# Attention and max-out FFN on one core: key tile 2 of batch 0 in one score group, whole value products, and batch 2's loads one pair later

## The chip, the cores and the metric

One core of a Trainium2 chip runs the whole program. The metric is the device time of one execution in microseconds (us). Engines are named as in the profile: PE multiplies matrices, ACT applies functions, DVE and POOL do elementwise work, SP issues transfers; POOL and ACT can issue transfers too.

## What is computed

Attention with 16 extra "beacon" keys and values in front, then a feed-forward network (FFN) whose hidden layer is the maximum of three products. B, H, S, Nb, D are 8, 8, 576, 16, 64; the FFN is 512 to 768 to 512 over 4608 tokens.

```python
k_all = concatenate([beacon_k, k], axis=2)       # 592 keys
v_all = concatenate([beacon_v, v], axis=2)
scores = matmul(q, k_all.T) / sqrt(D)            # causal over the 576, beacons always seen
a = exp(scores - scores.max(-1)); a /= a.sum(-1) + 1e-9
x = matmul(a, v_all)                             # heads side by side: (4608, 512)
h = maximum(maximum(x @ w1, x @ w2), x @ w3)
out = h @ w_out
```

## The kernel before, in words

**Tiling.** Two heads make a pair; there are four pairs per batch and 32 in all, and two pairs make a quad, whose four heads fill the 128 output partitions 32 by 32. The 592 keys are five tiles of 128 (the last has 80). Scores are kept transposed, keys on partitions, queries on columns; key tile t meets only queries from `q_min[t]` on (0, 112, 240, 368, 496). `exp` is taken without subtracting the maximum, the triangle of a tile is masked to zero, and a value product gives, for each quad, three "parts": part 0 multiplies by ones and gives the sums, parts 1 and 2 are the even and odd value columns. A part's columns from HEAD (64) to 576 fill one bank of 512 columns of the accumulator memory; its first 64 columns go to a shared fourth bank (`pv_heads`).

**Order of work.** The order is written out by hand; every engine runs its own instructions in that order. `first_batch` interleaves, for batch 0, the turning of queries and keys (`T`, L424), scores and their exps (`S_`, L506 and L515), masks (`M`, L563 on DVE), value products (`P`, i.e. `pv_rest`, L592) and the normalization: sums are inverted on ACT as Ln and Exp (`invert_rest`, L633, L634), for the first 64 columns on DVE (L628), and DVE multiplies (L639, L648) into `xT`, the FFN's input. Then the FFN's first units follow (`F_in`, L763). Batch 0's columns are worked on in halves of 288 (HALF), since its queries and keys are loaded in halves.

In batch 0 each pair has four score groups, a group being what one exp takes (`groups_0`, L70): group 0 holds tiles 2, 1 and 0 of the first half of the queries, groups 1 to 3 the rest. Tile 2 is therefore in two groups: 48 columns in group 0, 288 in group 3. Scores of group 0 run while half of the keys is absent, so those columns of the key tile are set to zero (L196). `EARLY` and `LATE` (L607) are the pieces of a part that `pv_rest` multiplies: tiles 0, 1, 2 for the first half, tiles 0 to 4 for the second.

`second_batch` handles pairs 4 to 7 (batch 1): `emit_burst` computes all four groups of a pair (L521) into pairs of banks chosen by `next_pairs`, exps are L541, masks L565 on POOL. Between them stand FFN units (L733, L750) and the turning of the next pair (L405). At its end `emit_pv_whole` multiplies quad 2 (L684) and ACT copies or inverts its banks (L694, L695, L700, L701); then the list of free banks is reordered: the banks of the sums and of the heads (`late_banks`) go to its end. The loop in `emit_all` then takes pairs 8 to 31 in the same way, with a `plan` of what is cast, stored and loaded at which pair.

**Loads.** Batch 0 and the pairs up to 9 are loaded and cast by POOL's queue (`load_cast`) or by SP into halves; from pair 10 on, and for all values, SP loads into seven staging buffers (`load_pair` L226, `load_v` L300 and L305) and POOL casts (L276, L321). `loads` is a list sorted by the step at which a load is cast. At pair 6, after its masks, `second_batch` takes five entries: the first waits for a small memset on POOL (L224), and the order is pair 10, pair 11, values of batch 2 in two pieces, pair 12. After that each cast releases the next load. Pair 10 is cast at pair 8, pair 11 and the first values at pair 9 (pair 11 first), the second values behind them.

## Time and profile before

| | us |
|---|---|
| three timed runs | 283.8, 285.6, 287.52 (median 285.6) |
| the profiled execution, its own time | 284.03 |
| its span from first to last instruction | 282.2 |
| PE busy in the span | 271.6 |
| ACT busy | 162.8 |
| first FFN matmul of batch 0 (L763) starts | 23.76 |
| last PE work ends | 278.6 |

The granted clock of PE is 0.999. The span is read from the left: up to about 24 us the core fetches its first inputs and works batch 0 with little to overlap; from there PE has FFN units to fill every gap until 278.6 us, and the last output is stored behind it. Times in the timeline are from the span's start.

### The profile page before, as it was taken

Reading aid. Unit: us, or ns where it says so; the run is one execution under the profiler, and the core shown is the slowest. Engines: PE = TensorE matmul, PEld = TensorE weight load, DVE = VectorE, ACT = ScalarE, POOL = GpSimd, SP = SyncE. Lnnn points to the kernel's source line nnn. Section 1 sums busy time; section 2 is a strip of 40 time slices with the busy share of each in tenths; the row PEclk is TensorE's granted clock in tenths of the full one; section 3 lists DMA queues with packets and bytes.
Section 4 is the critical chain, followed back from the end, with each engine's and each line's share of the span. In section 5 each row is a group of like instructions: output and inputs, shape, how many; then the busy total and the mean of one; then the engine's idle time right before and its main releaser. Section 6 shows DMA issues by size and latency. Waiting matters only on the chain.

```text
span 282.2 us, 7689 instructions
## 1 busy us (share of the span) xinstructions
PE 271.6 (96%) x3020; PEld 156.4 (55%) x3050; DVE 171.1 (61%) x307; ACT 162.8 (58%) x307; POOL 133.0 (47%) x273
## 2 busy tenths in 40 slices
PE   7788999999999999999999999999999999999994
PEld 3557765556555555555556886555555554444442
DVE  4885655574837566464737382638363847876872
ACT  4995797978668566756675758585857540000000
POOL 7194378557286946475557655683245300000000
PEclk9999999999999999999999999999999999999999
DMA  8999989989997999999999999979745003003004
GB/s 145 214 180 204 219 159 159 241 200 293 275 205 229 199 241 245 186 249 207 250 194 189 252 243 242 187 161 236 184 105 172 0 2 149 2 1 149 0 0 149
DMA packets 85315, 48.82 MB, mean 173 GB/s; under 512 B 64416, under 2 KB 80032, under 8 KB 85280
## 3 DMA queue, kind: packets, MB, share of 16 engines
q1 hardware_dynamic: 78320, 42.25, 66.7%
q0 software_dynamic: 6544, 5.80, 13.5%
q8 instruction: 23, 0.38, 0.6%
q10 hardware_dynamic: 416, 0.30, 0.4%
q14 instruction: 12, 0.10, 0.1%
HBM read 35.13 MB, written 14.22 MB: 175 GB/s over the span
## 4 chain that ended last, share of the span: by engine, by line
PE 92%; ACT 4%; DVE 2%; issue 1%; DVEq 0%
PE acc L733 46%; PE acc L786 16%; PE acc L684 11%; PE acc L521 8%; PE acc L763 4%; ACT at_sb L515 4%; PE acc L405 2%; PE acc L465 1%; PE acc L592 1%; PE acc L804 0%; PE acc L506 0%; PE acc L424 0%; DVE kT L432 0%; DVE hT L750 0%; DVE busy L184 0%
## 5 line engine op out<-in xcount | busy, mean ns | idle before, releaser
L733 PE MATMUL acc<-xT,w_sb 128*128 128x512 bf16 (+4 forms) x728 | 134.2, 335 | 1.5 <-issue 0.2
L750 DVE TENSOR_TENSOR hT<-hT,acc 128x512 bf16<-128x512 bf16 (+1 forms) x104 | 70.2, 677 | 62.5 <-PE acc L733 55.2
L733 PEld LDWEIGHTS <-w_sb 128*128 128x128 bf16 x752 | 69.8, 98 | 59.5
L565 POOL TENSOR_SCALAR_AFFINE_SELECT at_sb<-at_sb 128x256 bf16<-128x256 bf16 x168 | 61.1, 385 | 81.5 <-ACT at_sb L541 80.8
L541 ACT ACTIVATE at_sb<-acc 128x208 bf16<-128x208 f32 (+3 forms) x140 | 89.6, 735 | 5.2 <-PE acc L521 3.3
L786 PE MATMUL acc<-w_out_sb,hT 128*128 128x512 bf16 (+2 forms) x241 | 48.3, 348 | 0.3
L752 ACT CAST hT<-acc 128x352 bf16<-128x352 f32 x18 | 8.1, 452 | 46.9 <-PE acc L733 46.9
L276 POOL CAST p<-st 96x768 bf16<-96x768 f32 x44 | 35.0, 824 | 0.0
L786 PEld LDWEIGHTS <-hT 128*128 128x128 bf16 x246 | 22.6, 98 | 22.0 <-DVE hT L750 1.9
L793 DVE COPY y<-acc 128x512 f32<-128x512 f32 (+1 forms) x35 | 22.0, 629 | 20.8 <-PE acc L786 15.2
L752 DVE CAST hT<-acc 128x512 bf16<-128x512 f32 (+1 forms) x48 | 26.6, 554 | 9.6 <-PE acc L733 9.1
L811 ACT COPY y<-acc 128x320 f32<-128x320 f32 x1 | 0.4, 426 | 46.0 <-PE acc L804 46.0
L521 PE MATMUL acc<-qT,kT 64*128 64x208 bf16 (+1 forms) x336 | 26.3, 279 | 0.2 <-DVE hT L750 0.2
L684 PE MATMUL acc<-at_sb,v_sb 128*32 128x336 bf16 (+5 forms) x672 | 22.8, 281 | 0.0
L521 PEld LDWEIGHTS <-kT 64*128 64x128 bf16 x336 | 15.4, 94 | 11.5 <-issue 1.1
L711 DVE TENSOR_TENSOR xT<-raw,recip 128x576 bf16<-128x576 f32 x28 | 20.7, 781 | 0.9 <-ACT recip L548 0.9
L321 POOL CAST v_sb<-st 128x1536 bf16<-128x1536 f32 (+2 forms) x21 | 18.3, 897 | 0.0
L684 PEld LDWEIGHTS <-v_sb 128*32 128x32 bf16 (+1 forms) x672 | 14.4, 97 | 6.6
L694 ACT COPY raw<-acc 128x512 f32<-128x512 f32 x28 | 15.7, 633 | 2.8 <-PE acc L684 2.8
L684 PE MATMUL acc<-at_sb,ones 128*32 128x512 bf16 (+3 forms) x336 | 14.9, 284 | 0.0
L515 ACT ACTIVATE at_sb<-acc 128x1024 bf16<-128x1024 f32 (+3 forms) x16 | 12.6, 864 | 0.8 <-PE acc L506 0.8
L763 PE MATMUL acc<-xT,w_sb 128*128 128x256 bf16 x96 | 11.7, 273 | 0.0
(76 smaller groups left out, 174.5 us busy)
## 6 DMA issues: line engine op xcount, KB each, us to landing
out_dram<-y SPq DMA_DIRECT2D x35, 256.0 KB, 3.4
st<-in_q_dram SPq DMA_DIRECT2D x22, 288.0 KB, 4.6
st<-in_k_dram SPq DMA_DIRECT2D x22, 288.0 KB, 5.1
st<-in_v_dram SPq DMA_DIRECT2D x24, 256.0 KB, 5.8
w_sb<-in_moe_w_dram POOLq DMA_DIRECT2D x6, 384.0 KB, 8.6
q_dram<-p SPq DMA_DIRECT2D x16, 144.0 KB, 2.5
k_dram<-p SPq DMA_DIRECT2D x16, 144.0 KB, 2.4
st<-in_v_dram SPq DMA_DIRECT2D x8, 224.0 KB, 6.1
```

The source lines that it names most:

```text
L276: cast(t16.rearrange("p r h d -> p h r d"), st[0:QP, i * NQ2 : (i + 1) * NQ2].rearrange("p (h r d) -> p h r d", h=2, r=QR),)
L515: nc.scalar.activation(out=both_heads(p, gi), in_=ps[:, :, 0 : g_width(p, gi)], func=AF.Exp, scale=scale)
L521: nc.tensor.matmul(ps, kTs[p % NT][hs, 128 * t : 128 * t + 128], qTs[p % NT][hs, q0:q1], start=True, stop=True, tile_position=(64 * e, 0),)
L541: nc.scalar.activation(out=both_heads(p, gi)[:, e0:e1], in_=acc[:, first + e0 : first + e1, 0 : g_width(p, gi)], func=AF.Exp, scale=scale,)
L565: nc.gpsimd.affine_select(out=view, in_=view, compare_op=ALU.is_ge, fill=0.0, base=x0, pattern=[[0, 2], [1, hi - lo]], channel_multiplier=-1,)
L684: nc.tensor.matmul(acc[32 * j : 32 * j + 32, bank, lo + q0 - qa : lo + qb - qa], lhsT, at_view(PPQ * quad + j // 2, t, j % 2, q0, qb), sta ...
L733: nc.tensor.matmul(ps[:, a:b], w_in[i][:, ct, 128 * ft : 128 * (ft + 1)], xT[:, ct, x0 : x0 + b - a], start=(ct == 0), stop=(ct == n_ct - 1),)
L750: nc.vector.tensor_max(h[:, lo:hi], h[:, lo:hi], ps[:, lo:hi])
L752: (by_act if hi < TOKB else by_dve)(h[:, lo:hi], ps[:, lo:hi])
L763: nc.tensor.matmul(ps, w_in[i][:, ct, 128 * (ft + f) : 128 * (ft + f + 1)], xT[:, ct, tb * TOKB + lo : tb * TOKB + hi], start=(ct == 0), s ...
L786: nc.tensor.matmul(ps[:, lo:hi], hT[:, ft, 128 * tt : 128 * (tt + 1)], w_out_sb[:, ft, lo:hi], start=(ft == 0), stop=(ft == n_ft - 1),)
L793: (by_act if hi < d_model else by_dve)(y[:, lo:hi], ps[:, lo:hi])
```

## The change

In batch 0, group 0 keeps tiles 1 and 0 (464 columns a head instead of 512) and group 3 takes tile 2 whole (416 instead of 368); the zeroing of the key columns is gone. `EARLY` and `LATE` are cut anew: tile 0 is one piece of 512 columns, tile 1 two pieces, tiles 2 to 4 one each. In `first_batch` the products follow that: quad 1's parts 1 and 2 are each multiplied whole, with the multiply of that part's early columns behind it, and quad 0's late products of tile 3 and 4 move ahead of quad 1's.

Batch 2's loads are taken at pair 7, after its masks, and no longer at pair 6, and the second cast of batch 1's values goes ahead of them. Their order becomes pair 10, values, pair 11, pair 12, and pair 11 is cast behind both value pieces. The reordering of the banks at the end of `second_batch` is dropped.

```diff
     groups_0 = [
-        [(2, q_min[2], HALF), (1, q_min[1], HALF), (0, 0, HALF)],
+        [(1, q_min[1], HALF), (0, 0, HALF)],
         [(0, HALF, S)],
         [(1, HALF, S), (3, q_min[3], S)],
-        [(2, HALF, S), (4, q_min[4], S)],
+        [(2, q_min[2], S), (4, q_min[4], S)],
     ]
...
-        nc.vector.memset(z[:, Nb + HALF : 384], 0.0)
...
-    EARLY = [(0, HEAD, HALF), (1, q_min[1], HALF), (2, q_min[2], HALF)]
-    LATE = [(t, max(HALF, q_min[t]), S) for t in range(n_kt)]
+    EARLY = {0: (HEAD, S), 1: (q_min[1], HALF)}
+    LATE = {1: (HALF, S), **{t: (q_min[t], S) for t in range(2, n_kt)}}
...
+    BEHIND_V = 2 * PPB + 3
+
     def cast_step(p):
-        return (p - 2, 0) if p < B_PE * PPB else (p - 5, int(p < 19))
+        return (p - 2, int(p == BEHIND_V)) if p < B_PE * PPB else (p - 5, int(p < 19))
...
-    loads = [(cast_step(p), 2 * (p >= B_PE * PPB), partial(load_turned_pair, p)) for p in range(2 * PPB + 2, NPAIR)]
+    loads = [
+        (cast_step(p), 2 * (p >= B_PE * PPB or p == BEHIND_V), partial(load_turned_pair, p))
+        for p in range(2 * PPB + 2, NPAIR)
+    ]
...
-        P(0, (0,), (0, 1, 2))
+        P(0, (0,), (0, 1))
...
-        P(0, (0,), (), (0, 1, 3))
+        P(0, (0,), (), (1, 3))
...
-        P(0, (1, 2), (2,), (0, 1))
+        P(0, (1, 2), (), (1, 2))
         S_(3, 3)
         M(2, 3, True)
         M(3, 3, True)
-        P(0, (1, 2), (), (2,))
+        P(0, (1, 2), (), (3,))
         first = sc_psum.tile()
         open_pv(1, first[:, 0], sc_psum.tile(), first[:, 1])
-        P(1, (0,), (0, 1, 2))
+        P(1, (0,), (0, 1))
         pv_heads(1)
-        P(1, (0,), (), (0, 1, 3))
+        P(1, (0,), (), (1, 3))
+        P(0, (1, 2), (), (4,))
         P(1, (0,), (), (2, 4))
-        P(1, (1, 2), (0, 1, 2))
...
         multiply_heads(1)
-        for i in range(2):
-            multiply_rest(1, HEAD, HALF, i, i + 1)
-        P(1, (1, 2), (), (0, 1, 2))
-        for quad in range(n_quad):
-            P(quad, (1, 2), (), (3,))
-        for quad in range(n_quad):
-            P(quad, (1, 2), (), (4,))
+        for part in (1, 2):
+            P(1, (part,), (0, 1), (1, 2, 3, 4))
+            multiply_rest(1, HEAD, HALF, part - 1, part)
...
             if p == PPB + 2:
+                cast_v(1, 1, by_pool)
+            if p == PPB + 3:
                 next_load(gate=nc.gpsimd)
                 next_load(4)
-                cast_v(1, 1, by_pool)
...
-        for i in late_banks:
-            free_banks.remove(i)
-            free_banks.append(i)
         return finish
...
     for p in range(2 * PPB + 2, B_PE * PPB):
-        at_step(*cast_step(p), C(cast_pair, p, by_pool, by_pool))
+        if p != BEHIND_V:
+            at_step(*cast_step(p), C(cast_pair, p, by_pool, by_pool))
     for b in range(2, B):
         for i in range(2):
             at_step(*v_step(b, i), C(cast_v, b, i, by_pool))
+    at_step(*cast_step(BEHIND_V), C(cast_pair, BEHIND_V, by_pool, by_pool))
```

More of the change, by code (lines that the diff above doesn't have):

```diff
@@ L614, in pv_rest @@
                 for t in ts:
-                    _, q0, q1 = spans[t]
-                    pv_matmuls(
-                        quad,
-                        part,
-                        bank[:, q0 - HEAD : q1 - HEAD],
-                        t,
-                        q0,
-                        q1,
-                        t == 0,
-                        t == len(spans) - 1,
-                    )
+                    q0, q1 = spans[t]
+                    out = bank[:, q0 - HEAD : q1 - HEAD]
+                    pv_matmuls(quad, part, out, t, q0, q1, t == 0, t == n_kt - 1)
     def invert_heads(quad):
@@ L652, in multiply_rest @@
         )
-    late_banks = []
     def emit_pv_whole(quad, order=(0, 1, 2, 3), split=False):
@@ L662, in emit_pv_whole @@
         banks = [banks[i] for i in order]
-        late_banks[:] = [banks[0], banks[3]]
         every = range(n_kt)
```

## The prediction

> **What bounds the kernel now.** I read the page's busy line and chain shares first, then the chain of waits in order of time, then the timeline by engine around the two places that the change touches (13 to 31 us and 42 to 70 us), then the landing times of the transfers there.

> ```profile
> PE 271.6 (96%) x3020; PEld 156.4 (55%) x3050; DVE 171.1 (61%) x307; ACT 162.8 (58%) x307; POOL 133.0 (47%) x273
> ...
> PE 92%; ACT 4%; DVE 2%; issue 1%; DVEq 0%
> ```

> PE (the matmul engine) is busy for 96% of the span and is 92% of the chain that ended last. From about 24 us to 278 us the chain is almost unbroken PE work, so the end moves by what is gained or lost before 24 us, and by any new PE stall afterwards. The chain of waits shows the part before 24 us:

> ```profile
> 9.36 10.57 ACT at_sb L515 x14
> ...
> 19.95 0.39 DVE at_sb L563 x2
> 20.34 0.47 DVE recip L628
> ...
> 21.48 0.38 DVE xT L648
> 21.86 0.04 issue
> 21.90 1.01 PE acc L592 x27
> 22.91 0.26 issue
> 23.16 0.66 PE acc L592 x27
> 23.83 2.73 PE acc L763 x24
> ```

> Columns: start, length, what. ACT's 14 last exps of batch 0 run back to back to 19.93; DVE masks the last of them and multiplies early columns of batch 0 (L648); only then may PE write the late columns into the same banks (L592, 21.90), and the FFN starts at 23.83. The PE timeline names that wait, and one at pair 8:

> ```profile
> 21.90 1.01 PE L592 MATMUL acc<-at_sb,v_sb 128*32 128x288 bf16 x27 [0.90 <-DVE xT L648]
> ...
> 50.55 1.01 PE L521 MATMUL acc<-qT,kT 64*128 64x464 bf16 x10 [0.21 <-DVE hT L750]
> ```

> The loads of batch 2 (POOL gate and casts, then SP's queue):

> ```profile
> 45.58 0.10 POOL L224 MEMSET st<- 96x1 f32 x1
> ...
> 46.74 1.86 POOL L565 TENSOR_SCALAR_AFFINE_SELECT at_sb<-at_sb 128x256 bf16<-128x256 bf16 x6
> ...
> 48.22 11.31 SPq L305 DMA_DIRECT2D st<-in_v_dram  x5
> ```

> The gate is at 45.58, pair 7's masks end at 48.60, and SP is held 11.31 us by five value loads.

> **Part 1: batch 0 (the main term).** Columns streamed stay the same; 12 groups of four value or sum products vanish (in each of two quads and three parts, 224+288 becomes 512 and 48+288 becomes 336), and 8 score matmuls of 48 columns.
> What a group costs beside its columns: the two parts of tiles 0 and 1 run from 16.68 to 17.14, 0.46 us for 800 columns in 4 groups; at 2.4 columns per ns (row L684: two parts of 1600 columns in 52.18 to 53.55) that is 0.333 us of streaming, so 32 ns per group. L684's own row leaves 4 ns. I take 32, from the same line.
> [...]

> When do the exps end? Each of the first four shrinks from 1024 to 928 columns and each of the last group's grows from 736 to 832. Starts of a 1024 and of a 576 are followed by the next 0.92 and 0.58 us later, so 96 columns are 0.073 us. The first exps save about 0.2 us in all before 11 us (two shortened, and the score matmuls ahead 0.06 sooner); the last four give back 0.29. That alone is +0.09. But PE now streams 1376 instead of 800 columns between scores (3,1) and (3,2): +0.24 us, so (3,2) starts at about 17.38 instead of 17.14 and its exp at 17.78 instead of 17.57. From there 2.36 us as before plus 2 x 0.073: the last exp ends at 20.25 to 20.3 instead of 19.93. I take 20.25.

> Then: mask of pair 3, 0.02 + 0.44 (0.39 before; a 128x256 mask is 332 ns, a 128x160 one 322) to 20.7. PE has by then done all that does not need it: scores (3,3) can start near 18.8, when exp (3,2) frees their banks, and take 0.3; the ten groups behind them take about 1.2 us, to 20.3. Last sums to 20.8. Quad 1's two parts, six groups each of 1600 columns together: 0.667 + 6 x 0.032 = 0.86 us each, to 22.5. The old wait of 0.90 is gone because no product follows a multiply in its bank. Late next is the multiply of part 2, which now waits for that part's last product: about 0.1 + 0.35 us, to 22.95. The first FFN unit needs it only for its fourth matmul; three take 0.35 us from 22.5, so the loss is about 0.15 and the FFN starts in effect at 22.65. **-1.2 us** against 23.83.

> The recip chain is not in the way: four ACT steps took 19.79 to 21.42, so they end at about 21.9, before part 2 is done. Nor is the second half of the first FFN weights: issued at 14.84 on POOL, landing 7.3 us, 22.14, and POOL resumes on it at 22.41; this is the floor. Bounds: -1.75 (exps at 20.02, 4 ns per group) and -0.6 (the 0.26 issue gap stays, the part-2 multiply costs its full 0.45).

> The four removed memsets of 92 ns on DVE lie before a 2.39 us wait for the first load: nothing; without that cover 0.2 us. The four removed masks free DVE about 0.9 us in 11 to 17 us, before the wait for the last exp: nothing.

> **Part 2: no bank reordering.** Pair 8's second score group used banks 6 and 7, whose closing FFN unit DVE releases at 50.5: the 0.21 wait. Now it takes banks 2 and 3, released by ACT's L694 and L700 at about 49.97, and banks 6 and 7 come last. From pair 8 on the two assignments are one another's relabelling. PE gains up to 0.21, but ACT runs without a pause from 50.42 to 61.45 and pair 9's scores (57.27) stand right behind its key copy (57.28): **-0.1 us** (0 to -0.21).

> **Part 3: the loads of batch 2.** The gate memset moves behind the second cast of batch 1's values and pair 7's masks: 48.65 - 1.2 = 47.45, so issues start at about 47.6 instead of 45.70, 1.9 us later by the clock and 3.1 us later against their users, who come 1.2 us earlier. Nothing else waits in SP's queue: the first store is at 60.80, and five output buffers bear 2 to 3 us.
> Pair 10: keys issued at 48.0, landing 7.3 us as now, 55.3; their cast (0.82 us) ends at 56.1; PE turns the pair at 59.42 - 1.2 = 58.2. Spare 2.1 us.
> Values: behind pair 10 only, no longer behind pair 11. Now they land at 60.8 (49.4 + 11.4) and 62.8 (57.0 + 5.8); 1.9 us later less 1.1 for pair 11's two issues, 61.6 and 63.6. The casts (1.49 and 1.1 us) end at 63.1 and 64.7; PE needs the first tiles at 66.33 - 1.2 = 65.1 and the last two some 0.5 us later. Spare about 1 us.
> Pair 11 lands last, 62.8 + 1.9 = 64.7 at worst; cast 1.6 us to 66.3; PE turns it at 68.76 - 1.2 = 67.5. Spare 1.2 us. Pair 10's masks stand behind that cast on POOL, up to 1.5 us late; their products come at about 80. The skipped cost is **0**, hidden by these spares; each us beyond them would be a us of PE.
> Pair 9 and the output weights (12.0 to 13.1 and 11.3 us to landing, against 3.7 to 4.9 for pair 8 just before batch 2's loads began) should land sooner. Pair 9's keys now arrive at 54.8 for a turn at 55.14, so no wait goes, but one is kept from arising.

> **Sum.** -1.2 - 0.1 + 0 = -1.3 us. The profiled execution took 284.03 (span 282.2), so 282.7 on its scale. It is 1.6 under the median of the three timed runs (285.6); all four times have a mean of 285.2. A new median will more likely lie about that mean: **283.9 us**.

> **Rivals.**
> - *Nothing gained (0.18).* The work saved before 20 us waits for the exps anyway, the exps end later, and a PE gap such as the 0.26 "issue" reappears before the FFN. For: ACT is the chain there. Against: 0.90 of waiting and quad 0's late products leave the tail after the last mask. If the FFN starts at 23.8, 285.2.
> - *Slower: pair 10's load is late (0.12).* Its landing is 7.3 us now; if it takes 13.1, as pair 9's keys did in the same crowd, it lands at 61.1, its cast ends at 61.9, and PE waits 3.7 us at 58.2. It decides from a landing of 9.4 us on. For: it is issued 3.1 us later against its user. Against: pair 9 and the output weights are then nearly done, and a load at 59.57 lands in 4.5. 283.9 + 3.7 = 287.6.
> - *Larger gain (0.08).* The lower bound of part 1 with the full 0.21: 285.2 - 1.95 = 283.3 or less.
> - The change doing something else than it says is no case: the order of instructions shows it on PE, POOL and SP.

> **How the numbers follow.** Forecast 0.62 (its own range 282.9 to 284.9), nothing gained 0.18, late load 0.12, larger gain 0.08. The four times before lie within 1.9 of their mean, so the range is 281.9 to 286.4: it holds the first, second and fourth case with that scatter and leaves out the late load. About 2% (5.7 us) is what a measurement of this kernel can tell from no change; no gain here comes near it (0.02), and the late load reaches it only with more than one such stall (0.04); within 2% 0.94.

> **What would show it.** Right: the last exp near 20.2, no wait of L592 for L648, the first L763 at 22.4 to 22.9, no wait at pair 8's second group, turns of pairs 10 and 11 without a wait. Wrong: L763 at 23.5 or later; L405 waiting for a cast near 58 or 67; L684 waiting for values near 65.

## The result and the profile after

The changed kernel took 283.1 us (median of 22, 282.2 to 284.93) beside 284.57 for the kernel before (22 runs, 283.41 to 288.58): a ratio of 0.9948, 95% interval 0.9929 to 0.9968, or 1.47 us less. Forecast: 283.9, from a sum of -1.3 on a time before of 285.2; of the 0.8 us that it is off, 0.6 is this base. The profiled execution took 283.08 with a span of 281.4 (284.03 and 282.2 before).

Two lines of the page of the changed kernel, busy time and chain shares:

```profile
PE 273.4 (97%) x2994; PEld 156.1 (55%) x2994; DVE 171.1 (61%) x299; ACT 162.8 (58%) x307; POOL 131.5 (47%) x273
...
PE 92%; ACT 5%; DVE 1%; issue 0%
```

PE still carries the chain. The chain of waits through batch 0's tail (start, length, what):

```profile
9.95 6.25 ACT at_sb L514 x8
...
17.48 0.70 PE acc L591 x16
18.17 0.34 PE acc L505 x4
18.51 0.02 issue
18.53 2.52 ACT at_sb L514 x3
...
21.07 0.30 DVE at_sb L562
21.38 0.04 issue
21.42 1.75 PE acc L591 x52
...
23.19 0.40 DVE xT L639
23.59 0.04 issue
23.64 2.45 PE acc L751 x21
26.09 0.20 PE acc L360 x4
```

Two things are to be seen. The wait for a multiply between value products (0.90 before) and the 0.26 "issue" are gone; behind the mask stand the last products (1.75) and then the FFN, whose first three matmuls run beside the multiply. And the exps no longer run through: between 16.2 and 18.5 the chain goes over PE, whose 16 products of 512 columns (17.48) stand ahead of the score that ACT waits for.

Absolute times mislead here. In this execution the exps begin at 9.95, 0.59 later than in the one before, though nothing ahead of them changed by so much: two of PE's opening 320-column matmuls took 0.53 us instead of 0.27, so PE was at half rate around 5 us. So I measure from the first of the unbroken exps to the end of the first FFN unit, less that unit's 2.73 us: 26.56 - 2.73 - 9.36 = 14.47 before, 26.09 - 2.73 - 9.95 = 13.41 after. **The stage is 1.06 us shorter**: exps +0.53 (10.57 to 11.10), what follows the last exp -1.59 (3.90 to 2.31).

Further on, PE's weight loads can be laid beside the same ones of the kernel before. From pair 9's scores to the end the lead of the changed kernel grows by another 0.16 us near 105 us and by 0.21 near 175 us, and stays the same elsewhere. 1.06, 0.16 and 0.21 make 1.43, close to the 1.47 of the medians.

At pair 8, the timeline of PE after the change:

```profile
49.60 1.07 PE L520 MATMUL acc<-qT,kT 64*128 64x208 bf16 x12
...
55.40 1.47 PE L774 MATMUL acc<-w_out_sb,hT 128*128 128x352 bf16 x12 [0.41 <-ACT recip L688]
```

The 0.21 wait at pair 8 is gone; a wait of 0.41 for ACT's inversion stands 5 us later, and behind it PE's lead over the kernel before is what it was ahead of pair 8 (0.47 us by the clock). The queue that issues batch 2's values:

```profile
49.78 6.60 SPq L304 DMA_DIRECT2D st<-in_v_dram  x5
```

SP is held 6.60 us instead of 11.31, and neither PE nor POOL waits for a load of pairs 10, 11 or the values.

### The profile page after: what moved, and what is told of

It is laid out like the page before. It is cut to its first block, busy times and chain, and to the rows that moved or that the text cites. A ratio compares the mean times of both kernels' runs of the same rounds, so it can differ in the third digit from the quotient of the medians.

```text
span 281.4 us, 7592 instructions
## 1 busy us (share of the span) xinstructions
PE 273.4 (97%) x2994; PEld 156.1 (55%) x2994; DVE 171.1 (61%) x299; ACT 162.8 (58%) x307; POOL 131.5 (47%) x273
## 4 chain that ended last, share of the span: by engine, by line
PE 92%; ACT 5%; DVE 1%; issue 0%
PE acc L721 47%; PE acc L774 16%; PE acc L672 10%; PE acc L520 8%; PE acc L751 4%; ACT at_sb L514 3%; PE acc L404 2%; PE acc L464 2%; PE acc L591 1%; ACT at_sb L540 1%; PE acc L505 1%; PE acc L792 0%; PE acc L423 0%; ACT recip L688 0%; ACT raw L682 0%
## 5 line engine op out<-in xcount | busy, mean ns | idle before, releaser
L721 PE MATMUL acc<-xT,w_sb 128*128 128x512 bf16 (+4 forms) x752 | 135.7, 336 | 0.0
L738 DVE TENSOR_TENSOR hT<-hT,acc 128x512 bf16<-128x512 bf16 (+1 forms) x104 | 70.1, 677 | 61.5 <-PE acc L721 54.8
L564 POOL TENSOR_SCALAR_AFFINE_SELECT at_sb<-at_sb 128x256 bf16<-128x256 bf16 x168 | 60.0, 377 | 82.0 <-ACT at_sb L540 81.9
L781 DVE COPY y<-acc 128x512 f32<-128x512 f32 (+1 forms) x35 | 21.9, 628 | 20.9 <-PE acc L774 14.0
L672 PE MATMUL acc<-at_sb,v_sb 128*32 128x336 bf16 (+5 forms) x672 | 22.8, 281 | 0.0
L514 ACT ACTIVATE at_sb<-acc 128x928 bf16<-128x928 f32 (+3 forms) x16 | 12.6, 865 | 1.7 <-PE acc L505 1.7
```

The costliest lines, as they stand in the source:

```text
L564: nc.gpsimd.affine_select(out=view, in_=view, compare_op=ALU.is_ge, fill=0.0, base=x0, pattern=[[0, 2], [1, hi - lo]], channel_multiplier=-1,)
L672: nc.tensor.matmul(acc[32 * j : 32 * j + 32, bank, lo + q0 - qa : lo + qb - qa], lhsT, at_view(PPQ * quad + j // 2, t, j % 2, q0, qb), sta ...
L721: nc.tensor.matmul(ps[:, a:b], w_in[i][:, ct, 128 * ft : 128 * (ft + 1)], xT[:, ct, x0 : x0 + b - a], start=(ct == 0), stop=(ct == n_ct - 1),)
L738: nc.vector.tensor_max(h[:, lo:hi], h[:, lo:hi], ps[:, lo:hi])
L781: (by_act if hi < d_model else by_dve)(y[:, lo:hi], ps[:, lo:hi])
```

## The experiments: one part at a time

**Batch 0 alone** (the kernel before with the batch 0 part of the diff).

> The kernel before with the batch 0 part alone (groups, pieces, order of the products); loads and bank order as before. Theory 1 (the gain is the end of batch 0: no product waits for a multiply in its bank, quad 0's late products move ahead): 1.2 to 1.6 us faster than before, the whole of what was measured. Theory 2 (the gain is the transfers: pair 9 and the output weights land sooner, and the earlier FFN alone would run into them): 0 to 0.5 us, with the turn of pair 9 waiting. Theory 3 (the gain is pair 8's bank order): 0.

Measured: 283.12 (12 runs) beside 284.46; ratio 0.9964 [0.9933, 0.9994], -1.34 us by the medians. Its chain has the same shape: last exps at 18.13, FFN at 23.23, 13.50 us by the measure above, -0.97.

**Loads alone**, and **everything but the loads**.

> The kernel before with the load part alone (batch 2's loads at pair 7, values first). Theory 1: within 0.3 us of before. Theory 2: 0.8 to 1.5 us faster. A cost hidden in the loads would show as slower, with casts of pair 10 or 11 late.

> The changed kernel with the load part undone (batch 2's loads at pair 6, pair 11 ahead of the values). Theory 1: as the changed kernel, 1.2 to 1.6 us faster than before. Theory 2: slower than the changed kernel by 0.8 us or more.

Measured: 284.98, ratio 1.0037 [1.0009, 1.0066]; and 283.63, ratio 0.9972 [0.9939, 1.0005]. The first says that the loads cost 0.5 us, the second (against 283.1 for the whole change, measured at another time) that they gain 0.5. Both profiled executions had a low mean clock (0.988 and 0.987), and with the loads alone PE comes to the same weight load of batch 0 1.87 us later (19.81 instead of 17.94, by the count below); among executions with a clock of 0.994 or more the median spans are 282.5 beside 282.5 for before, and 280.9 beside 281.2 for the whole change. I chose this selection after the fact, but the two signs oppose each other with it or without. So I take the loads as worth 0, within about 0.3.

**Banks alone.**

```diff
-        for i in late_banks:
-            free_banks.remove(i)
-            free_banks.append(i)
```

> The kernel before without the bank reordering, nothing else. Theory 1: the wait of 0.21 us at pair 8's second score group goes, ACT takes it back by pair 9's scores, 0 to 0.1 us faster. Theory 3: 0.4 us faster or more, kept to the end.

Measured: 284.23, ratio 1.0006 [0.998, 1.0033]. The wait at pair 8 goes and the one for ACT comes, as in the whole change:

```profile
56.36 1.47 PE L786 MATMUL acc<-w_out_sb,hT 128*128 128x352 bf16 x12 [0.41 <-ACT recip L700]
```

**Can that be had back?** Quad 3's products in another bank order, and pair 9's query copy on DVE:

```diff
-            finish = emit_pv_whole(p // 2 - 1) if p % 2 == 0 else None
+            finish = emit_pv_whole(p // 2 - 1, (2, 0, 1, 3) if p == 2 * PPB else (0, 1, 2, 3)) if p % 2 == 0 else None
...
-                    turn_pair(p + 1, by_act)
+                    turn_pair(p + 1, by_dve if p == 2 * PPB else by_act)
```

> The changed kernel with quad 3's value products filled in the bank order 2, 0, 1, 3 and pair 9's query copy on DVE instead of ACT. Theory 1 (ACT's work between quad 3 and pair 9 takes back what the missing wait at pair 8 gave): no wait of 0.41 us on L688 before burst 9, and none instead of it, -0.4 us against the changed kernel. Rival (DVE or the next bank is late instead): the wait moves to another releaser and the time stays, 0.0 (+0.2 if DVE's multiply of the tail then comes late).

Measured: 285.06, ratio 1.0001 [0.9969, 1.0033]; not -0.4 but 1.5 us worse than the changed kernel, by the two ratios. The same edit on top of the next experiment's kernel gave 283.93 beside 282.61, measured together, +1.32; its PE timeline names the place:

```profile
52.02 0.86 PE L672 MATMUL acc<-at_sb,ones 128*32 128x512 bf16 x20 [1.31 <-ACT at_sb L540]
...
57.97 0.88 PE L520 MATMUL acc<-qT,kT 64*128 64x208 bf16 x12 [0.17 <-DVE qT L438]
```

The new order gave the sums, which are multiplied first, a bank that an exp of the same pair was still reading. My rival "the next bank is late" was the right one, at 1.3 us and not the 0.0 to 0.2 that I gave it.

## The experiments: why the tail is shorter

**The split parts.**

```diff
-        P(0, (1, 2), (0, 1))
+        P(0, (1,), (0, 1))
         S_(3, 2)
+        P(0, (2,), (0, 1))
         S_(2, 3)
```

> The changed kernel with part 1's two groups of quad 0 left ahead of the score (3,2) and part 2's moved behind it. Theory 1 (ACT's 0.34 us stall on that score is the price of the merge and lies on the chain): the stall shrinks to 0.05 or less, the last exp ends 0.3 us sooner and so does the FFN: -0.3 us against the changed kernel. Rival (PE's products of the tail bound the stage, not the exps): the last exp ends sooner and the FFN does not, 0.0.

Measured: 282.61 (9 runs) beside 284.99, ratio 0.9917 [0.9884, 0.9949], the lowest median of this study. The chain:

```profile
9.31 10.73 ACT at_sb L514 x14
...
20.06 0.30 DVE at_sb L562
...
20.40 1.75 PE acc L591 x51
...
22.62 2.45 PE acc L751 x21
25.07 0.20 PE acc L360 x4
```

The 14 exps are one piece again, and the stage takes 25.07 - 2.73 - 9.31 = 13.03 us, 0.38 less than in the changed kernel: ACT's stall was on the path. (The intervals of the two ratios overlap; the 0.38 is the profile's.) With the edit on quad 3 on top:

> The changed kernel with both edits: the parts of quad 0 split around score (3,2), and quad 3's bank order with pair 9's query copy on DVE. If both theories hold the gains lie at different places of the PE chain and add: -0.7 us against the changed kernel, -2.1 against before. If either rival holds, -0.3 to -0.4; if both, 0.

Measured: 283.93, ratio 0.996 [0.9933, 0.9986], for the reason shown above.

**The tail's order alone**, with tile 2 in two pieces as before.

```diff
+        P(0, (1, 2), (), (3,))
...
+        P(0, (1, 2), (), (4,))
...
-        for i in range(2):
-            multiply_rest(1, HEAD, HALF, i, i + 1)
...
+        for part in (1, 2):
+            P(1, (part,), (0, 1, 2), (0, 1, 2, 3, 4))
+            multiply_rest(1, HEAD, HALF, part - 1, part)
```

> The kernel before with the order of batch 0's tail alone changed: quad 0's tiles 3 and 4 go ahead, and each part of quad 1 is finished whole with its multiply behind it; key tile 2 stays in two pieces, the banks and the loads as before. Theory 1 (the gain comes from the tail order; merging tile 2 costs about 0.4 us net): exps take 10.6 us from their unbroken start as before, the FFN follows the last exp after 2.3 us plus four more groups of 0.03 = 2.4 instead of 3.9, so -1.4 us against before, 283.1 if before stands at 284.5. Theory 2 (the merge carries the gain, by fewer groups and fewer exp columns at the start): -0.5 us or less, 284.0 or more, with the FFN 3.3 us or more after the last exp.

Measured: 284.63, ratio 1.0 [0.9965, 1.0035]. Theory 1 seems to fall. But the chain shows what ate the gain:

```profile
19.65 2.43 PE acc L592 x98
22.07 1.66 issue
23.74 0.87 PE acc L592 x23
...
24.63 0.40 DVE xT L648
...
25.07 2.45 PE acc L763 x21
27.53 0.20 PE acc L361 x4
```

1.66 us in which PE waits for nothing that the profile shows, early in part 2. The exps start at 9.80 here; without the gap the stage would be 27.53 - 2.73 - 1.66 - 9.80 = 13.34, an estimate. A gap at the same place, 28 weight loads ahead of the FFN's first, stood in the kernel before (0.26) and in the loads-alone kernel (0.45). The DMA part of the page has two queues of the kind "instruction"; in the kernel before, the line of the busier one (packets, MB, share) is:

```profile
q8 instruction: 23, 0.38, 0.6%
```

I take it for PE's, since its packets keep step with PE's count: 23 packets of 16 KB for about 6,100 PE instructions (3,050 weight loads, and a matmul behind each), 265 for each packet; and from the packet at 11.18 to the one at 244.42, the 22nd after it, PE starts 2,785 weight loads, 253 instructions for each. By estimate, then, pages of about 256. Asked in windows of 0.2 us, the packet next ahead of the gap lies at 20.8 to 21.0 in the kernel before, 21.2 to 21.4 here and 22.8 to 23.0 with the loads alone; PE goes on at 23.16, 23.74 and 25.20, **2.2 to 2.4 us behind the start of the packet each time**. Counted by weight loads, PE was 256 instructions ahead of the gap at 17.94, 18.47 and 19.81, so by this estimate the page is there 5.2 to 5.4 us after PE enters the one before it (the expectations below reckon with 5.1). The theory that I tested: a page is asked for on entering its predecessor, and is late when the 128 matmuls pass in less than that; here they take 3.6. All fourteen traces fit at this border, as reckoned: the packet starts 1.0 to 3.2 us behind PE's entry into the page ahead, never before it, and PE passes the border no sooner than 2.2 us behind the packet. The banks-alone kernel, with the same instructions up to here, seems to have no gap (0.01 by its chain), but that is a matter of modelled ends: its 56 last products take 0.26 us more than those of the control below, which does not meet the border there.

**Moving the page border.** The opening matmuls on constant data, whose results nothing uses, are cut into more and smaller ones, which shifts everything behind them on PE's instruction queue:

```diff
-        keep_busy(8, 480)
+        keep_busy(72, 44, rows=32)
```

> The tail-order kernel with PE's 8 opening matmuls on constant data (480 columns each) cut into 72 of 44 columns (32 weight columns): 64 more weight loads and 64 more matmuls, 128 instructions, ahead of all else on PE's queue, results unused as before. Theory (PE's instructions arrive in pages of 256; the page that begins 57 instructions before the first FFN matmul is asked for when PE enters the page ahead of it and is there 5.1 us later): the page borders move to 185 before and 71 behind the first FFN matmul, where PE arrives after the page, so the 1.66 us gap is gone, the FFN starts 2.4 us after the last exp, and the time is 1.5 us below the tail-order kernel, about 283.1. Rival (the gap belongs to that place in the work, a datum or a bank that is late without a record): the gap stays at the same matmul and the time at 284.6.

> The same with 40 opening matmuls of 80 columns, 64 more instructions. Page theory: the border moves to 121 instructions (60 matmuls) before the first FFN matmul; PE would come there at about 21.2 on the tail-order kernel's clock and the page is there at about 22.4, so a gap of about 1.2 us stands 60 matmuls before the FFN instead of 1.66 us 29 before it, and the time is 0.3 to 0.5 us below the tail-order kernel, 284.2. Rival: a gap of 1.66 us, 29 matmuls before the FFN, 284.6.

> The kernel before with the same 72 opening matmuls of 44 columns, as a control. Page theory: the 0.26 us issue gap ahead of the FFN goes and nothing else, -0.26 us against before. Rival: the gap stays, 0.0. If the cut opening matmuls themselves cost something, the first scores come later and the time rises in both theories.

> The changed kernel with 64 opening matmuls of 48 columns, 112 more instructions: exactly as many as the change took from batch 0, so the page border is back at 57 instructions before the first FFN matmul. Page theory: PE takes 5.0 us for the 128 matmuls up to that border here (3.6 in the tail-order kernel) and the page 5.1, so a gap of 0.1, at most 0.3 us, and 283.1 to 283.4: the merge pays for itself by thinning out that stretch, not by where the border falls. Rival (a border ahead of the FFN costs its gap wherever it is met): a gap of 1 us or more, 284.2 or more.

Measured: medians 285.77, 285.15, 285.78 and 285.55 beside 285.1; ratios 0.9977 [0.9935, 1.002], 0.9985 [0.995, 1.0021], 0.9986 [0.9945, 1.0028] and 0.9987 [0.9946, 1.0028]. As medians the first three miss the times of both theories, and the fourth meets its rival's (284.2 or more); but they tell nothing of the border, because many executions were slower from the start: in three of the four profiled ones (all but the control's) PE was at half rate long into batch 0. Two 288-column score matmuls took 0.42 us, at 12.37 with 128 more instructions and as late as 19.64 in the changed kernel with 112 more, beside 0.30 in the kernel before; in the kernel with 64 more, whose granted clock was 0.50 up to 20 us, the stretches read (busy by engine, then PE's clock, DMA share, GB/s):

```profile
8.00:12.00 4.00, 3.69 (x56) 1.97 (x50) 2.37 (x10) 2.90 (x3) 0.00 (x0) 0.50 1.33 211
12.00:20.00 8.00, 7.69 (x113) 3.90 (x111) 6.16 (x24) 6.49 (x10) 6.93 (x12) 0.50 1.10 191
```

Whether the cut matmuls caused this isn't shown: the kernel before, with its 8 uncut ones, took 285.3 us or more in 17 of the 35 executions measured beside these, the control in 6 of 12.

The lowest times still speak, though no trace of these executions is kept, and though those of the kernels without the cut matmuls, but for the kernel before, were measured at another time, on another chip or on one not recorded. Tail order with 128 more instructions: three of 12 at 282.22 to 282.40, where the lowest of the tail order without them is 283.97: **-1.75 us** for the same work with another page border (expected -1.5 from the page, 0 from the rival; the lowest of the kernel before was 283.75 beside the one and 283.45 beside the other, so time and chip don't make the gain). Tail order with 64 more: 283.37, or -0.6 (expected -0.3 to -0.5 from the page, 0 from the rival). The control's four lowest lie at 283.57 to 283.71, beside 283.75 for before. The changed kernel with 112 more: 282.36 and 282.81, where without them the two lowest are 282.20 and 282.51. By these four times a border ahead of the FFN costs it no more than about 0.3 us, as the page theory had it, and not 1 us.

The control's profiled execution was not slowed, its exps start at 9.36 as in the kernel before, and its chain can be laid beside that kernel's:

```profile
22.01 1.42 PE acc L592 x56
23.43 2.73 PE acc L763 x24
26.16 0.20 PE acc L361 x4
```

The 56 products run in one piece and the 0.26 is gone; the stage is 14.07, 0.40 less. Here the rival fails: all behind the opening matmuls is as in the kernel before, and only the border has moved. The same 56 products in the PE timelines of the control and of the banks-alone kernel:

```profile
22.01 1.42 PE L592 MATMUL acc<-at_sb,v_sb 128*32 128x288 bf16 x56 [0.90 <-DVE xT L648]
...
22.64 1.68 PE L592 MATMUL acc<-at_sb,v_sb 128*32 128x288 bf16 x56 [0.90 <-DVE xT L648]
```

In the kernel before they take 1.01 + 0.26 + 0.66 = 1.93 us, so the border there goes with 0.51 us, more than the 0.26 that the chain calls "issue". The control's instruction packet lies at 15.0 to 15.2 instead of 20.8. In the kernel with 64 more, PE came to its border only at about 23.7, when the page was due: no gap of 1.2 us, and no test.

## Why the prediction was right, step by step

- *Batch 0, -1.2.* The part alone gives -1.34 by the medians and -0.97 by its profile; the stage in the whole change -1.06. Size right.
- *Last exp +0.32.* Measured +0.53. I moved the score (3,2) 0.24 later for the columns ahead of it; from the exps' start it is 0.38 later (8.16 instead of 7.78 us), since the score (3,1) ahead of those columns was already 0.13 late, which I had not reckoned with. ACT stood for 0.34. The split-parts kernel shows that this was avoidable.
- *From the last exp to the FFN 2.4.* Measured 2.31, by the steps named: mask, sums, two parts, and a multiply beside the first FFN matmuls.
- *32 ns for a group of four.* Too much. PE streams 2.4 columns per ns: in the kernel before, FFN matmuls of 512 columns start 215 ns behind one another and those of 256 columns 109, so 256 columns take 106 ns. Quad 1's two parts start at 21.57 and the FFN at 23.09, 1.52 us for 12 groups and 1.333 us of streaming: 16 ns each. With 16 groups (tail order, 128 more instructions) they take 24.74 to 26.27, 1.53 us: 12 ns. I took the 32 from two parts in batch 0; L684's row, which leaves 4, was nearer, and the groups that the merge saves are worth next to nothing on PE. The error is 12 x 0.016 = 0.19. Of the whole step it leaves 0.09 (2.31 instead of 2.4), and that much of the 0.21 missing on the exps is made good by luck.
- *The 0.26 issue gap* stood only in a bound; the sum had it gone without a reason, and that it went was luck. By the page theory it was a late instruction page, and its end carries more than I knew: tail order without the page problem 13.34 by the estimate above, whole change 13.41, and the lowest times are 282.22 and 282.20, so by these merging tile 2 gains nothing by its work. It costs the exps 0.5 us, and pays, by the same theory, because 112 fewer PE instructions keep the page out of the way: in the changed kernel's trace PE passes this border 3.1 us after the FFN's first matmul and 4.3 us behind its packet.
- *Banks, -0.1.* The mechanism, ACT taking it back, is shown at 55.40, and there it takes back all. The medians give -0.23, the ratio 1.0006 with an interval around 1. A stall of about 0.16 us near 105 is also gone in the profiles of the kernels without the reordering and stands in those with it; the prediction did not name it.
- *The total.* 0.37 of the 1.43 us that the profile shows, near 105 and near 175, lies where the prediction named nothing, and it more than makes up for what batch 0 fell short of -1.2. That part of the agreement is luck. The 0.21 near 175 is missing in the banks-alone kernel and in the control and present in the tail-order kernel; its cause was not looked for.
- *Loads, 0.* No transfer was late; worth 0 within 0.3. The late-load rival did not happen.
- *Rivals.* "Nothing gained" did happen, in the tail-order kernel, and by its own words: a gap that reappears before the FFN. The merge kept it from the change. The measured 283.1 lies under the 283.3 of "larger gain", but only because the kernel before came out at 284.57 and not at 285.2; the gain is 1.47 and not 1.95.
- *The range.* The four times before lie within 2.3 us of their mean; 1.9, from which the range was made, is the distance from their median.

What stays open: how far ahead of its use a page is asked for was inferred from places and times, not seen; and whether the crowd of transfers at 15 to 24 us delays it was not tried. Why some executions stay at half rate until about 20 us (a clock of 0.50 in the kernel with 64 more instructions) is open too.

## What to carry to other kernels

An "issue" gap at the same instruction count in several variants may be a late instruction page: count PE's instructions (weight loads too), look for the instruction packet ahead of the gap (it started 2.2 to 2.4 us before PE went on here), and move the border to test it. Where the 128 matmuls ahead of the border, by the estimate, passed in 3.6 us, the gap was 1.66 us, and where they took 5.0 it was 0.26; so thin out a stretch of many small matmuls, or let the border fall elsewhere. Where an engine's next input waits behind a block of products, put only half of the block ahead of it (here 8 products instead of 16), and check which exp still reads a bank before changing the order in which banks are filled.
